# A transformer-style block in fp32: the second normalisation as a factor per token on the turned first one

## The chip, the cores and the metric

The kernel runs on one core of one Trainium2 chip. The metric is the device time of one execution in microseconds (us), as the median of several runs. A core has five instruction streams that run beside each other and meet only at semaphores: PE (matmuls; PEld is its loading of weights), DVE (vector work), ACT (activations, copies), POOL (a second vector engine, without access to the matmul accumulators in PSUM) and SP, which here issues every transfer (DMA). Each stream runs its instructions strictly in order, so an instruction that waits holds up everything behind it on its engine.

## The reference, cut to what matters

The shapes are 2048 tokens, 512 features, 32 heads of 16, a window of 256 keys and 1792 hidden features.

```python
def _layernorm(x, axis=-1, eps=1e-5):
    m = jnp.mean(x, axis=axis, keepdims=True)
    v = jnp.var(x, axis=axis, keepdims=True)
    return (x - m) / jnp.sqrt(v + eps)

x  = A_x
xn = _layernorm(x)
s  = attention(xn, A_wqkv, window=256) @ A_wo          # causal, softmax over 256 keys
y  = _layernorm(xn)                                    # a second normalisation, of xn
h  = gelu(y @ B_w1 + B_b1)                             # 512 -> 1792
g  = silu(h @ B_w2 + B_b2)                             # 1792 -> 512
out = x + s * g
```

Since xn has mean 0 and variance v/(v+eps) for each token, y is xn times one number per token, 1/sqrt(v/(v+eps)+eps).

## The kernel before, in words

Matmuls run in fp32 split into a high and a low part: a product is three matmuls (high·high, high·low, low·high), and so every operand exists twice, as `hi` and `lo`. The normalised input is kept turned (features on partitions, tokens along the row) in one big tile, `big[:, part, kt, token]`, named xnT in the profile: part 0 is high, part 1 low, kt is the group of 128 features.

**Attention (up to about 426 us).** The heads go in 8 groups of 4 (n = 0 to 7), the keys of a group in 16 blocks. One pass of the loop over `t` (here called slot t) handles key block t: two score matmuls into the one buffer `stb` (named so in the profile, one for p = 1, one for p = 0), an exp of each on ACT into `pt`, two masks of each on POOL (AFFINE_SELECT), the row maximum for a block 12 slots later (`xy` on PE, then COPY_PREDICATED and TENSOR_REDUCE on DVE), and the product with the values (`zo<-pt,vt`) of the block before. From slot 116 on there are no maxima left, and the scores of p = 1 go to the buffer `xy`. The pairs of `stb` matmuls can be counted from the first at 62.20 us, two a slot, which gives the time at which each slot starts.

Other matmuls are hung into the slots by a table of numbers: `tandem(t0, t1, one, two)` lays two products of 512 columns, each cut into 64-row halves, over the slots t0 to t1, and they end in the two banks `fb`. These are the projections of the later head groups (`pair_qk`, shown as fb<-xnT,wqb), the values of the second half (`pair_v`), and ten of the fourteen hidden blocks of the first 512 tokens (`pair_h`, f = 6 to 13, 2 and 3). `at(t, ...)` puts an instruction into slot t, and `behind(t, ...)` at its end. Each engine's order is the order in which the code issues.

**The second normalisation.** The tokens go through the second half of the block in four chunks of 512. For chunk 0, `open_y` fetches xn back from DRAM (written there as `xn_d` at the start), `y_steps` take statistics and scale in slots 77 to 89, and `y_turn` turns the four tiles on PE in slots 91 and 92 (16 transposes) and splits them. For chunk 1, xn comes back from `xn_d`; for chunks 2 and 3 the input x is loaded again and normalised twice. These three are turned by DVE in 32x32 blocks (STREAM_TRANSPOSE), written to `z_d` and fetched back in pieces of 128 bytes.

**The MLP (426.6 us on).** Chunk c multiplies hidden blocks f with `w2` into four accumulators `acc`. For each f in `activate`, ACT takes the gelu, ACT casts it to its high part `gh` and DVE subtracts to get the low part `gl`; there are two buffers of each, so the cast for f waits for the end of PE's product of f-2. In chunk 1 PE alternates product i-1 with hidden block i+3 in step i, 5.44 us a step, until the hidden blocks run out after step 10; then products 10, 11, 12 and 13 follow each other in 2.72 us each. In steps 10 to 13 DVE and ACT also build the inputs for chunks 2 and 3 (`second_y`: seven sums and differences of the two chunks, which are then multiplied by seven combinations of `w1`: a Strassen-like scheme). From 568 us the two last chunks run.

Of the kernel before, what the change touches and what calls it, by code (L numbers as in the profile page):

```python
# [9 lines left out]
F32 = mybir.dt.float32  # L10
# [40 lines left out]
def mixer_kernel(ctx, tc, x, wqk, wv, wo, w1, b1, w2, b2, out):  # L51
# [7 lines left out]
    small = ctx.enter_context(tc.tile_pool(name="small", bufs=3))  # L59
    dram = ctx.enter_context(tc.tile_pool(name="dram", bufs=1, space=bass.MemoryType.DRAM))  # L60
    attn = ExitStack()
    psum = attn.enter_context(tc.tile_pool(name="psum", bufs=1, space=PSUM))
# [19 lines left out]
    def layernorm(ts, name, on_act, eager=False, n_act=4, by_sums=(), end_act=False, apart=()):  # L82

        n = len(ts)
        nm = small.tile([P, n], F32, tag="nm", name=f"nm{name}") if by_sums else None
        sums = small.tile([P, n, 2], F32, tag="sums", name=f"sums{name}") if by_sums else None

        def total(i):

            nc.scalar.activation(x23[:, 8], ts[i], AF.Identity, accum_out=sums[:, i, 0:1])
            nc.gpsimd.tensor_scalar(nm[:, i: i + 1], sums[:, i, 0:1], -1.0 / D, None, op0=ALU.mult)

        def squares(i):

            nc.scalar.activation(x23[:, 8], ts[i], AF.Square, bias=nm[:, i: i + 1], accum_out=sums[:, i, 1:2])
            ve = small.tile([P, 1], F32, tag="ve1", name=f"ve{name}_{i}")
            nc.gpsimd.tensor_scalar(ve, sums[:, i, 1:2], 1.0 / D, EPS, op0=ALU.mult, op1=ALU.add)  # L100
            nc.gpsimd.tensor_tensor(rs[:, i: i + 1], ve, mhalf[:, :1], op=ALU.pow)
# [7 lines left out]
        mv = small.tile([P, n, 2], F32, tag="mv", name=f"mv{name}")  # L109
        rs = small.tile([P, n], F32, tag="rs", name=f"rs{name}")  # L110
        sh = small.tile([P, n], F32, tag="shift", name=f"shift{name}")

        def each(i):

            stats(i)
            ve = small.tile([P, 1], F32, tag="ve1", name=f"ve{name}_{i}")
# [8 lines left out]
        def shift(i):  # L125
            nc.vector.scalar_tensor_tensor(sh[:, i: i + 1], mv[:, i, 0:1], -1.0, rs[:, i: i + 1],
                                           op0=ALU.mult, op1=ALU.mult)

        def stats(i):
            st = small.tile([P, 6], F32, tag="bn", name=f"bn{name}_{i}")  # L130
            nc.vector.bn_stats(st, ts[i])
            nc.vector.bn_aggr(mv[:, i], st)

        def invert():
            ve = small.tile([P, n], F32, tag="ve", name=f"ve{name}")
            nc.vector.tensor_scalar(ve, mv[:, :, 1], EPS, None, op0=ALU.add)
            nc.gpsimd.tensor_tensor(rs, ve, mhalf[:, :n], op=ALU.pow)

        def shift_all():
            if on_act:  # L140
                nc.vector.scalar_tensor_tensor(sh, mv[:, :, 0], -1.0, rs, op0=ALU.mult, op1=ALU.mult)

        def apply(i, on_act=on_act):
            if on_act:
                nc.scalar.activation(ts[i], ts[i], AF.Identity, bias=sh[:, i: i + 1], scale=rs[:, i: i + 1])
            else:
                nc.vector.tensor_scalar(ts[i], ts[i], mv[:, i, 0:1], rs[:, i: i + 1],
                                        op0=ALU.subtract, op1=ALU.mult)

        def end(i):  # L150

            if i < n_act:
                shift(i)
            apply(i, i < n_act)
        if eager:
            return [(lambda i=i: total(i), lambda i=i: squares(i), lambda i=i: end_sums(i)) if i in by_sums else
                    (lambda i=i: each(i), lambda i=i: end(i)) for i in range(n)]
        return [lambda i=i: stats(i) for i in range(n)] + [invert, shift_all] + [lambda i=i: apply(i) for i in range(n)]
# [23 lines left out]
    xn_d = dram.tile([8, P, D], F32, name="xn_d")  # L182
# [6 lines left out]
    z_d = dram.tile([NCH - 1, 4, P, 512], F32, name="z_d")  # L189
# [48 lines left out]
    b1s = const.tile([P, NF], F32, name="b1s")  # L238

# [123 lines left out]
    def pair_qk(n, c):  # L363
# [11 lines left out]
        def finish(ps, t, copy):  # L375
# [18 lines left out]
            free = t if (n, c) == (1, 2) else max(t + 1 + 2 * (c % 2), 16 * n - 28 + 4 * c)  # L394
            free += 2 * (t == 90)
# [29 lines left out]
    def pair_h(f):  # L425
# [98 lines left out]
    def max_rows(n, c, t):  # L524

        mt = mts.pop((n, c))
        mh = small.tile([P, 2, 2, 2, 4], F32R, tag="mh", name=f"mh_{n}_{c}")
# [4 lines left out]
        mT = small.tile([P, 32], F32, tag="mT", name=f"mT_{n}_{c}")  # L532
# [71 lines left out]
    def open_y():  # L604

        t = bigp.tile([P, 4, 512], F32, tag="wa", name="y0")
        mlp["y"] = [t[:, i] for i in range(4)]
        for i in range(4):
            nc.sync.dma_start(mlp["y"][i], xn_d[i])
        mlp["ln"] = layernorm(mlp["y"], "C0", False)  # L610
# [5 lines left out]
    W1_AREA = {6: 6, 7: 8, 8: 10, 9: 12, 10: 14, 11: 1, 12: 3, 13: 5, 2: 7, 3: 9, 0: 11, 1: 13, 4: 15}  # L616

    def open_yy():
        yh = bigp.tile([P, 2, 512], F32R, tag="wb0", name="yh")
        mlp["yy"] = ([yh[:, 0], yh[:, 1], area(4)[:, 0:512], area(4)[:, 512:1024]],  # L620
                     [area(j)[:, 512 * k: 512 * (k + 1)] for j in (0, 2) for k in range(2)])

    def open_w1():
        mlp["w1"] = bigp.tile([P, 2 * 512], F32R, tag="wb1", name="w1_5")

    def w1_part(a, f):
        at = area(W1_AREA[f]) if f in W1_AREA else mlp["w1"]
# [35 lines left out]
    def y_steps(a, b):  # L663
        run(mlp["ln"][a:b])

# [4 lines left out]

    def y_turn(kt):

        for i in range(4):
            nc.tensor.transpose(fb[kt % 2][:, P * i: P * (i + 1)], mlp["y"][i][:, P * kt: P * (kt + 1)], ident)
        split(mlp["yy"][0][kt], mlp["yy"][1][kt], fb[kt % 2])
# [31 lines left out]
    ln = layernorm(xs[0], "A0", True, True, 3)  # L707
# [8 lines left out]
    ln1 = layernorm(xs[1], "A1", True, True, 2, by_sums=(0, 1), end_act=True, apart=(3,))  # L716
    ln2 = layernorm(xs[2], "A2", True, True, by_sums=(0,))
    ln3 = layernorm(xs[3], "A3", True, True, by_sums=range(4))
# [14 lines left out]
    for i in range(8):  # L733
        behind(-14 + i // 4, nc.sync.dma_start, xn_d[i], xs[i // 4][i % 4])
# [20 lines left out]
    for n, spans in enumerate((((9, 14), (15, 19)), ((20, 24), (25, 30)), ((31, 35), (36, 41)), ((42, 47), (48, 53, 51)),  # L755
                               ((75, 79), (80, 84)), ((85, 90), (93, 98))), 2):
# [4 lines left out]
    for f, *span in ((6, 99, 104, 102), (8, 105, 110), (10, 111, 115), (12, 116, 121, 118, 119), (2, 122, 127, 124, 125)):  # L761
# [13 lines left out]
    at(88, open_yy)  # L775
    for kt in range(KT):
        fills.setdefault((91 + kt // 2, kt % 2), []).append((y_turn, (kt,)))
# [4 lines left out]
    at(99, open_w1)  # L782
    for f, t in ((6, 91), (7, 91), (8, 92), (9, 94), (10, 94), (11, 99), (12, 99), (13, 101), (2, 101), (3, 103), (0, 103),
                 (1, 105), (4, 105), (5, 107)):
        at(t, fetch, "w1", f)
    for f, t, lo_at, lo_by in ((6, 94, 95, nc.vector), (7, 95, 97, on_pool), (8, 96, 98, on_pool), (9, 97, 99, nc.vector),
                               (10, 100, 102, nc.vector), (11, 102, 103, nc.vector), (12, 103, 105, on_pool),
                               (13, 105, 106, on_pool), (2, 106, 108, nc.vector), (3, 107, 109, on_pool),
                               (0, 108, 110, on_pool), (1, 109, 112, nc.vector), (4, 111, 113, on_pool),
# [18 lines left out]
    def first_h(f):  # L808
# [4 lines left out]
        (nc.scalar.copy if f else nc.vector.tensor_copy)(ready[f], fb[f])  # L813
# [93 lines left out]

    def load_y(c):
        return load_x(c, ((mlp["yp"], "y"),), "y")

    def turn_y(c, tiles):

        for i in tiles:
            y = mlp["y"][i]
            nc.vector.transpose(y, y)
            nc.sync.dma_start(z_d[c - 1, i], y)

    def fetch_y(c, kt, dst):

        for k in range(4):  # L920
            at = z_d[c - 1, 0, 0, 128 * kt + 32 * k: 128 * kt + 32 * k + 32]
            nc.sync.dma_start(dst[32 * k: 32 * k + 32].rearrange("p (t j) -> p t j", j=32),
                              bass.AP(tensor=at.tensor, offset=at.offset, ap=[[512, 32], [32 * 512, 16], [1, 32]]))
# [38 lines left out]
    def end_chunk(c, accs, os_, between):  # L962
# [10 lines left out]
        for i in range(4):  # L973
# [16 lines left out]
            else:  # L990
                for q in range(2):
# [9 lines left out]
    halves_of = {("11", 0): 11, ("11", 1): 13, ("21", 0): 7, ("21", 1): 9, ("22", 0): 15, ("t1", 0): 6, ("t3", 0): 8,  # L1001
                 ("t2", 0): 10, ("t4", 0): 12, ("22", 1): 14, ("t1", 1): 1, ("t3", 1): 3, ("t2", 1): 5, ("t4", 1): 4}
# [349 lines left out]
```

## Time and profile before

| what | value |
|---|---|
| median of 3 runs | 738.41 us (738.13 to 738.72) |
| the profiled execution | 738.76 us, span of its core 737.0 us, granted clock 0.999 |
| busy | PE 98%, DVE 69%, ACT 60%, POOL 40% of the span |
| attention up to | 426.57 us (first `acc` matmul) |
| chunk 0 | 426.57 to 480.97 us |
| chunk 1 | 480.97 to 568.01 us |
| chunks 2 and 3 | 568.01 us to the end |

The span is the time from the core's first instruction to its last; 1.8 us lie around it. In the rows below a time is in us from the span's start. In a row of the timeline the first number is the start, the second the length, `x4` says that four like instructions are merged, and the bracket gives the idle time of that engine before it and what ended it. Line numbers are all L43, since one helper issues everything; the names of the tiles tell the work apart.

### The profile page before, as it was taken

Reading aid. Unit: us, or ns where it says so; the run is one execution under the profiler, and the core shown is the slowest. Engines: PE = TensorE matmul, PEld = TensorE weight load, DVE = VectorE, ACT = ScalarE, POOL = GpSimd, SP = SyncE. Lnnn points to the kernel's source line nnn. Section 1 sums busy time; section 2 is a strip of 40 time slices with the busy share of each in tenths; the row PEclk is TensorE's granted clock in tenths of the full one; section 3 lists DMA queues with packets and bytes.
Section 4 is the critical chain, followed back from the end, with each engine's and each line's share of the span. In section 5 each row is a group of like instructions: output and inputs, shape, how many; then the busy total and the mean of one; then the engine's idle time right before and its main releaser. Section 6 shows DMA issues by size and latency. Waiting matters only on the chain.

```text
span 737.0 us, 18757 instructions
## 1 busy us (share of the span) xinstructions
PE 724.7 (98%) x7360; PEld 585.3 (79%) x7360; DVE 511.2 (69%) x790; ACT 444.1 (60%) x744; POOL 298.4 (40%) x644
## 2 busy tenths in 40 slices
PE   8999999999999999999999999999999999999997
PEld 7886777777878887777776688888888888888886
DVE  7886777877776778887772677656667855667823
ACT  7757777878777676788877756443643734541001
POOL 7413757867666565767877600120002000001102
PEclk9999999999999999999999999999999999999999
DMA  8633356766565525747724397747452322253701
GB/s 292 194 65 78 83 145 168 191 169 184 148 151 144 159 72 150 177 124 190 206 82 144 115 324 187 186 125 209 107 107 104 114 68 86 64 180 120 248 19 57
DMA packets 84697, 105.71 MB, mean 143 GB/s; under 512 B 37312, under 2 KB 37568, under 8 KB 84608
## 3 DMA queue, kind: packets, MB, share of 16 engines
q1 hardware_dynamic: 84608, 104.51, 50.5%
q8 instruction: 58, 0.95, 0.5%
q14 instruction: 31, 0.25, 0.1%
HBM read 54.53 MB, written 32.77 MB: 118 GB/s over the span
## 4 chain that ended last, share of the span: by engine, by line
PE 92%; ACT 3%; DVE 2%; DMA 1%; POOL 1%; issue 0%; SPq 0%; DVEq 0%; ACTq 0%
PE acc L43 21%; PE fb L43 19%; PE zo L43 13%; PE p L43 9%; PE stb L43 9%; PE s L43 6%; PE h L43 6%; PE xy L43 5%; PE pv L43 3%; ACT pt L43 3%; POOL pt L43 1%; DMA wvr<-in_wv_dram 1%; DVE xy L43 1%; DVE mt L43 1%; SPq L43 0%
## 5 line engine op out<-in xcount | busy, mean ns | idle before, releaser
L43 POOL TENSOR_SCALAR_AFFINE_SELECT pt<-pt 128x256 f32<-128x256 f32 x480 | 193.6, 428 | 126.0 <-ACT pt L43 123.5
L43 ACT ACTIVATE pt<-stb 128x768 f32<-128x768 f32 (+1 forms) x244 | 188.7, 773 | 42.7 <-PE stb L43 35.9
L43 DVE TENSOR_REDUCE mt<-xy 128x4 f32<-128x1024 f32 (+1 forms) x128 | 152.6, 1192 | 4.4
L43 DVE COPY_PREDICATED xy<-upper,zo 128x512 f32<-128x512 int32 x112 | 77.8, 695 | 69.0 <-PE xy L43 61.5
L43 POOL TENSOR_TENSOR xo<-xo,gated 128x512 f32<-128x512 f32 x15 | 19.9, 1330 | 234.9 <-DVE gated L43 195.8
L43 PE MATMUL fb<-xnT,wqb 64*128 64x512 f32 (+1 forms) x684 | 106.6, 397 | 0.0
L43 PE MATMUL zo<-pt,vt 128*17 128x128 f32 x2880 | 103.7, 275 | 0.3 <-POOL pt L43 0.3
L43 PE MATMUL stb<-qk 64*128 64x384 f32 (+1 forms) x488 | 95.3, 385 | 4.4 <-ACT pt L43 2.9
L43 PE MATMUL acc<-w,gh 128*128 128x512 f32 x320 | 98.5, 389 | 0.0
L43 PEld LDWEIGHTS stb<-qk 64*128 64x128 f32 x488 | 45.7, 183 | 48.8 <-ACT pt L43 39.4
L43 PEld LDWEIGHTS zo<-pt,vt 128*17 128x17 f32 x2880 | 67.5, 97 | 15.6 <-issue 5.0
L43 PEld LDWEIGHTS fb<-xnT,wqb 64*128 64x128 f32 (+1 forms) x684 | 64.4, 185 | 8.4 <-issue 0.6
L43 PEld LDWEIGHTS acc<-w,gh 128*128 128x128 f32 x320 | 60.1, 188 | 12.5
L43 PE MATMUL acc<-w,gl 128*128 128x512 f32 x160 | 62.3, 389 | 0.0
L43 PE MATMUL xy<-qk 64*128 64x256 f32 (+2 forms) x536 | 58.5, 291 | 0.2 <-DVE mt L43 0.2
L43 ACT COPY oraw<-zo 128x128 f32<-128x128 f32 x108 | 28.7, 266 | 39.1 <-PE zo L43 26.6
L43 PEld LDWEIGHTS xy<-qk 64*128 64x128 f32 x536 | 46.7, 185 | 7.0 <-issue 3.1
L43 ACT ACTIVATE gated<-acc 128x512 f32<-128x512 f32 x16 | 8.7, 596 | 59.3 <-DVE acc L43 59.3
L43 PE MATMUL s<-wos,ohl 128*128 128x512 f32 (+1 forms) x204 | 44.3, 377 | 0.0
L43 PEld LDWEIGHTS s<-wos,ohl 128*128 128x128 f32 x204 | 36.8, 188 | 7.1
L43 PEld LDWEIGHTS zo<-qk 64*128 64x128 f32 x448 | 37.5, 185 | 5.3 <-DVE xy L43 2.0
L43 ACT COPY p<-p 128x512 f32<-128x512 f32 x21 | 12.3, 585 | 48.6 <-PE p L43 41.2
(190 smaller groups left out, 1242.5 us busy)
## 6 DMA issues: line engine op xcount, KB each, us to landing
qk<-sh SPq DMA_DIRECT2D x128, 128.0 KB
qk<-pjr SPq DMA_DIRECT2D x64, 128.0 KB
oT_d<-oraw SPq DMA_DIRECT2D x32, 256.0 KB
w_d<-in_w_dram SPq DMA_DIRECT2D x14, 512.0 KB
x<-in_x_dram SPq DMA_DIRECT2D x16, 256.0 KB
or<-oT_d SPq DMA_DIRECT2D x16, 256.0 KB
w<-rden_d SPq DMA_DIRECT2D x16, 256.0 KB
xo<-in_x_dram SPq DMA_DIRECT2D x16, 256.0 KB
```

The source lines that it names most:

```text
L43: r = issue(*args, **kwargs)
```

## The change

The second normalisation is no longer computed from data. `mvs`, `sums` and `rss` keep the statistics of the first one for all 16 tiles of 128 tokens. `scale_parts` makes of them one factor per token with small POOL instructions in slots 54 to 70, DVE turns the 128x32 table in slot 72, it goes to DRAM as `s_d` and comes back spread over all partitions as `scales` (512 tokens along the row). The turned first normalisation in `big` is used as the input of `w1` directly:

- chunk 0 stays where it is in `big`; `w1`'s products are multiplied by `scales` when they leave PSUM. In the attention stage that takes the place of a copy for f = 12, 13, 2, 3, 0 and 1 (on DVE); f = 6 to 11 are copied as before and multiplied on POOL after the attention stage; f = 4 and 5 get a DVE multiplication.
- chunk 1: both parts of `big` are written to DRAM by 12 transfers of 512 KB for chunks 1 to 3 (`keep_xt`, slots 25 to 69), and fetched back; each of the 14 hidden blocks gets a DVE multiplication before its gelu.
- chunks 2 and 3: high and low part are fetched, added on POOL (`join`) and multiplied on DVE (`scale`).

All statistics, scalings and turnings of the second normalisation, the transfers of `xn_d` and `z_d`, and the reloading of x for chunks 2 and 3 are gone. The two slots of the transposes fall out, and the table is written anew: the products of head groups 6 and 7 and the first hidden blocks move by up to one slot, and each pair of them from slot 80 to 115 now takes six slots. `w1`'s parts lie at other places of `big`.

On PE, slot 91, row by row. `qk` are the head group's rows, `ident` the identity that turns, `pt` and `vt` probabilities and values. Before:

```order
L43 MATMUL stb<-qk_695 128x384 x2
L43 MATMUL xy<-qk_91 128x256 x4
L43 MATMUL fb_108<-ident,y_4661 128x128 x4
L43 MATMUL stb<-qk_695 128x384 x2
L43 MATMUL fb_109<-ident,y_4661 128x128 x4
L43 MATMUL zo<-qk_91 128x128 x4
```

and now:

```order
L43 MATMUL stb<-qk_682 128x384 x2
L43 MATMUL xy<-qk_94 128x256 x4
L43 MATMUL fb_111<-xnT,wqb_4973 128x512
L43 MATMUL fb_112<-xnT,wqb_4973 128x512
L43 MATMUL fb_111<-xnT,wqb_4973 128x512
L43 MATMUL fb_112<-xnT,wqb_4973 128x512
L43 MATMUL fb_111<-xnT,wqb_4973 128x512
L43 MATMUL fb_112<-xnT,wqb_4973 128x512
L43 MATMUL stb<-qk_682 128x384 x2
L43 MATMUL zo<-qk_94 128x128 x4
```

The eight transposes of the slot have gone, and the last six half products of a projection pair stand there.

On DVE, steps 12 and 13 of chunk 1 (`gl` is the low part of a gelu, `yt` and `y_21` are the sums and differences for the last chunks, xnT the places they are split to). Before:

```order
L43 TENSOR_TENSOR yt_1_8300<-xnT,gated 128x512
L43 TENSOR_TENSOR gl_12_8317<-g_12_8314,gh_12_8316 128x512
L43 TENSOR_TENSOR xnT<-xnT 128x512
L43 TENSOR_TENSOR xnT<-yt_0_8298,xnT 128x512
L43 TENSOR_TENSOR xnT<-xnT 128x512
L43 TENSOR_TENSOR xnT<-yt_1_8300,xnT 128x512
L43 TENSOR_TENSOR y_21_7959<-y_21_7959,yt_0_8298 128x512
L43 TENSOR_TENSOR y_21_7959<-y_21_7959,yt_1_8300 128x512
L43 TENSOR_TENSOR gl_13_8349<-g_13_8346,gh_13_8348 128x512
```

and now:

```order
L43 TENSOR_TENSOR yt_1_8121<-yh_3_8020,gated 128x512
L43 TENSOR_TENSOR g_12_8135<-h_12_8041,scales 128x512
L43 TENSOR_TENSOR gl_12_8139<-g_12_8135,gh_12_8138 128x512
L43 TENSOR_TENSOR xnT<-yh_2_8017,xnT 128x512
L43 TENSOR_TENSOR xnT<-yt_0_8119,xnT 128x512
L43 TENSOR_TENSOR xnT<-yh_3_8020,xnT 128x512
L43 TENSOR_TENSOR xnT<-yt_1_8121,xnT 128x512
L43 TENSOR_TENSOR y_21_7816<-y_21_7816,yt_0_8119 128x512
L43 TENSOR_TENSOR y_21_7816<-y_21_7816,yt_1_8121 128x512
L43 TENSOR_TENSOR g_13_8168<-h_13_8091,scales 128x512
L43 TENSOR_TENSOR gl_13_8172<-g_13_8168,gh_13_8171 128x512
```

Ahead of each `gl` now stands the multiplication by `scales`, whose result ACT's gelu of the same f reads.

On POOL, slot 54 (`pt_6_1` and `pt_6_0` are the masks of that slot). Now:

```order
L43 AFFINE_SELECT pt_6_1_3489<-pt_6_1_3489 128x2x128 x2
L43 MEMSET sv 128x32
L43 TENSOR_SCALAR sv<-sums 128x1 x7
L43 COPY sv<-mvs 128x4
L43 COPY sv<-mvs 128x2
L43 COPY sv<-mvs 128x3
L43 AFFINE_SELECT pt_6_0_3528<-pt_6_0_3528 128x2x128 x2
```

Before, the two masks stood next to each other; eleven small instructions have come between them.

The core of the diff:

```diff
@@ finish of pair_h
-            copy(raw, ps)
+            if 5 < f < 12:
+                copy(raw, ps)
+            else:
+                nc.vector.tensor_mul(raw, ps, scales)
@@ instead of open_y
+    def scale_parts():
+        def variance():
+            nc.gpsimd.memset(sv, 0.0)
+            for i in range(4 * NCH):
+                if i in squared:
+                    nc.gpsimd.tensor_scalar(sv[:, i: i + 1], sums[:, i, 1:2], 1.0 / D, None, op0=ALU.mult)
...
+        def ratio():
+            for _ in range(2):
+                nc.gpsimd.tensor_tensor(sv[:, 0: 4 * NCH], sv[:, 0: 4 * NCH], rss, op=ALU.mult)
+            nc.gpsimd.tensor_scalar(sv[:, 0: 4 * NCH], sv[:, 0: 4 * NCH], EPS, None, op0=ALU.add)
+        def power(c):
+            at = sv[:, 4 * c: 4 * c + 4]
+            nc.gpsimd.tensor_tensor(at, at, mhalf, op=ALU.pow)
+    def keep_xt(c, kt):
+        nc.sync.dma_start(xt_d[c - 1, kt], big[:, :, kt, 512 * c: 512 * (c + 1)].bitcast(F32))
-    def y_turn(kt):
-        for i in range(4):
-            nc.tensor.transpose(fb[kt % 2][:, P * i: P * (i + 1)], mlp["y"][i][:, P * kt: P * (kt + 1)], ident)
-        split(mlp["yy"][0][kt], mlp["yy"][1][kt], fb[kt % 2])
@@ the table
-                               ((75, 79), (80, 84)), ((85, 90), (93, 98))), 2):
+                               ((75, 79), (80, 85)), ((86, 91), (92, 97))), 2):
...
-    at(74, open_y)
-    for i, t in enumerate((77, 78, 81, 82, 83, 83, 85, 86, 87, 89)):
-        at(t, y_steps, i, i + 1)
...
+    at(54, variance)
+    at(56, ratio)
+    for c in range(NCH):
+        at(58 + 4 * c, power, c)
+    at(72, nc.vector.transpose, svT, sv)
...
+    for k in range(KT * (NCH - 1)):
+        behind(25 + 4 * k, keep_xt, 1 + k // KT, k % KT)
@@ after the attention stage
-    mlp["y"] = [load(mlp["yp"], "y", xn_d[4 + i], f"y_1_{i}") for i in range(4)]
+        for k in range(2 if f < 12 else 0):
+            nc.gpsimd.tensor_tensor(t[:, k], t[:, k], scales, op=ALU.mult)
@@ chunk 1 onwards
+    def fetch_xt(c, kt, dst):
+        nc.sync.dma_start(dst, xt_d[c - 1, kt, :, 1])
+        kept["high", c, kt] = load(mlp["yp"], "y", xt_d[c - 1, kt, :, 0], f"yh_{c}_{kt}")
+    def join(c, kt, dst):
+        to = kept.pop(("high", c, kt))
+        nc.gpsimd.tensor_tensor(to if c > 2 else dst, dst, to, op=ALU.add)
...
+    def scale(c, dst):
+        nc.vector.tensor_mul(dst, dst, gated[:, c - 2])
@@ activate
+            if f not in made:
+                nc.vector.tensor_mul(g, src, scales)
+                src = g
             nc.scalar.activation(g, src, AF.Gelu_apprx_tanh, bias=b1s[:, f: f + 1])
@@ steps of chunk 1
+                if i == 9:
+                    for kt in range(KT):
+                        join(3, kt, kept["y3", kt])
+                        scale(3, kept["y3", kt])
```

More of the change, by code (lines that the diff above doesn't have):

```diff
@@ L123, in power, with apply @@
             nc.gpsimd.tensor_tensor(rs[:, i: i + 1], ve, mhalf[:, :1], op=ALU.pow)
[L125 to L143, printed above, removed]
+        def apply(i, on_act):
             if on_act:
@@ L152, in end @@
             if i < n_act:
-                shift(i)
+                nc.vector.scalar_tensor_tensor(sh[:, i: i + 1], mv[:, i, 0:1], -1.0, rs[:, i: i + 1],
+                                               op0=ALU.mult, op1=ALU.mult)
             apply(i, i < n_act)
[L155 to L158, printed above, removed]
+        return [(lambda i=i: total(i), lambda i=i: squares(i), lambda i=i: end_sums(i)) if i in by_sums else
+                (lambda i=i: each(i), lambda i=i: end(i)) for i in range(n)]
     def run(steps):
@@ L812, in first_h @@
         ready[f] = t2.tile([P, 512], F32, tag="t2", name=f"hf_{f}")
-        (nc.scalar.copy if f else nc.vector.tensor_copy)(ready[f], fb[f])
+        nc.vector.tensor_mul(ready[f], fb[f], scales)
     ready = {}
@@ L1182, in mixer_kernel @@
                     for kt in range(KT):
[L1183 removed]
+                        fetch_xt(2, kt, kept[kt // 2][:, kt % 2])
+                    for k in range(2):
+                        fetch_scales(2 + k, gated[:, k])
+                if i in (5, 6):
+                    for kt in (2 * i - 10, 2 * i - 9):
+                        join(2, kt, kept[kt // 2][:, kt % 2])
+                if i in (7, 8):
+                    for kt in (2 * i - 14, 2 * i - 13):
+                        scale(2, kept[kt // 2][:, kt % 2])
                 if i in (8, 9):
```

176 lines of the change are left out of this document (75 added, 101 removed).

## The prediction

> **What bounds the kernel now.** I read the page's busy shares and its chain of waits first, then the busy time by stretches, then the chain in order of time, and at last the timelines of the places that the change touches.
>
> ```profile
> span 737.0 us, 18757 instructions
> PE 724.7 (98%) x7360; PEld 585.3 (79%) x7360; DVE 511.2 (69%) x790; ACT 444.1 (60%) x744; POOL 298.4 (40%) x644
> PE 92%; ACT 3%; DVE 2%; DMA 1%; POOL 1%; issue 0%; SPq 0%; DVEq 0%; ACTq 0%
> ```
>
> PE carries the chain, so the stages have to be looked at one by one. The chain from the MLP on:
>
> ```profile
> 527.21 2.72 PE h L43 x12
> ...
> 546.25 10.88 PE acc L43 x48
> ```
>
> and the busy time by stretches (columns: PE, PEld, DVE, ACT, POOL, granted clock, DMA share, GB/s):
>
> ```profile
> 62.00:275.73 213.73, 210.80 (x3352) 166.92 (x3350) 153.68 (x191) 159.05 (x267) 142.05 (x338) 1.00 0.55 143
> 426.57:480.97 54.40, 54.40 (x241) 45.06 (x241) 37.78 (x64) 29.97 (x49) 4.89 (x4) 1.00 0.76 222
> 480.97:568.01 87.04, 87.04 (x385) 72.10 (x385) 58.44 (x112) 42.88 (x68) 9.87 (x8) 1.00 0.51 134
> ```
>
> PE has not one gap in chunk 0 (54.40 us) and chunk 1 (87.04 us). There is nothing to win there by taking work from DVE, ACT or the transfers; such work can only be put in PE's way. Everything to be won lies in the attention stage. The slots there start with the first of two `stb` rows. The six starts below are those of slots 36, 54, 80, 98, 110 and 115; the other two rows are the transposes of slot 91.
>
> ```profile
> 165.93 0.44 PE L43 MATMUL stb<-qk 64*128 64x384 f32 x2 [0.20 <-ACT pt L43]
> 215.32 0.44 PE L43 MATMUL stb<-qk 64*128 64x384 f32 x2
> 290.23 0.44 PE L43 MATMUL stb<-qk 64*128 64x384 f32 x2
> 322.04 0.66 PE L43 MATMUL fb<-ident,y 128*128 128x128 f32 x4
> 323.16 0.66 PE L43 MATMUL fb<-ident,y 128*128 128x128 f32 x4
> 341.85 0.45 PE L43 MATMUL stb<-qk 64*128 64x384 f32 x2 [0.16 <-ACT pt L43]
> 375.19 0.38 PE L43 MATMUL stb<-qk 64*128 64x256 f32 x2
> 389.43 0.46 PE L43 MATMUL stb<-qk 64*128 64x384 f32 x2
> ```
>
> **The attention stage: the table.** Slots 80 to 114 (35 slots) take 389.43 - 290.23 = 99.20 us, 2.83 us each: the five or six slots of a pair are unevenly loaded, two of them hold transposes, and DVE and POOL do the second statistics. Afterwards each pair there takes six slots, which hold 8, 8, 8, 8, 10 and 6 half products. Before, slots 36 to 53 have that load three times over with nothing else in them: (215.32 - 165.93) / 18 = 2.744 us each. Slots 98 to 109 have it but for one slot's shift, with the preparation of `w1` beside it: (375.19 - 341.85) / 12 = 2.778 us. If all 35 slots go at 2.744, they take 96.04 us and 3.2 us are won. If slots 92 to 114, where `w1` is prepared, go at 2.778, it is 12 x 2.744 + 23 x 2.778 = 96.82, and 2.4 us are won. I take the middle, **-2.8 us**. The 16 transposes are part of this and not added to it.
>
> **The end of the attention stage.** At slot 121 ACT copies h of f = 12; now DVE multiplies it. The chain there:
>
> ```profile
> 405.35 0.47 ACT hr L43
> 405.83 0.73 ACT pt L43
> 406.61 0.86 POOL pt L43
> 412.98 0.41 PE zo L43 x8
> ```
>
> ACT's copy lies on the chain with 0.47 us, ahead of an exp and of a run of masks which ends at 412.98. It moves to DVE, where a multiplication out of PSUM follows another; the new wait would be PE's for the second bank, whose first use is in slot 122. I take **-0.4 us**, between 0 (the masks end as late) and -0.5. At slot 127 DVE was idle, and a second multiplication of some 0.7 us there, and those of f = 0 and 1, cost nothing as long as PE's twelve matmuls between them cover them.
>
> **POOL in slots 54 to 70.** The factors cost eleven small instructions in slot 54, three in 56, and four powers of 128x4.
>
> ```profile
> L43 POOL TENSOR_TENSOR rsC<-veC,mhalf 128x4 f32<-128x4 f32 x5 | 5.5, 1102 | 46.1 <-DVE veC L43 46.1
> L43 POOL TENSOR_SCALAR nmA<-sumsA 128x1 f32<-128x1 f32 x7 | 1.5, 223 | 7.1 <-ACT x L43 7.1
> 218.11 0.77 POOL L43 TENSOR_SCALAR_AFFINE_SELECT pt<-pt 128x256 f32<-128x256 f32 x2 [0.66 <-ACT pt L43]
> 220.85 0.95 PE zo L43 x28
> ```
>
> Eleven times 0.22 us is 2.45 us. POOL was idle 0.66 us before the masks at 218.11, so they slip by 1.8 us, from an end at 218.88 to 220.7. The first to wait for them is PE's `zo` at 220.85, whose last third alone reads them: **0 us**, and at most 0.5 if the small ones follow each other at 0.28. A power of 1.1 us exceeds such a pause by 0.5 us in a slot with as much slack again.
>
> **Transfers.** 12 x 512 KB leave in slots 25 to 69 (121 us at 2.74 a slot), 52 GB/s on top of the 143 at a share of 0.55. The head groups' rows that share SP's queue and the lanes are sent ten slots or more ahead of their use from group 3 on, and SP waits for nothing new there, so **0 us**; if one landing came late, its lateness would be the price, at most 2 us by the length of a transfer of this size. Gone are the eight writes of xn at the start; no chain ran through them, 0 us. In chunk 0, four loads of 512 KB replace sixteen of 128-byte pieces, and DVE and ACT lose their splits: nothing, since PE had no gap.
>
> ```profile
> 443.95 0.72 ACT L43 ACTIVATE g<-hr,b1s 128x512 f32<-128x512 f32 x1
> L43 POOL TENSOR_TENSOR xo<-xo,gated 128x512 f32<-128x512 f32 x15 | 19.9, 1330 | 234.9 <-DVE gated L43 195.8 <-DMA xo<-in_x_dram 37.2 <-issue 1.9
> ```
>
> The six POOL multiplications of f = 6 to 11 (1.33 us each by the row `xo`, 8 us from about 431 us on) end before the first gelu that needs them, at 443.95 us, unless the tiles land 4 us late.
>
> **Chunk 1, the tail.** Here the change adds 14 multiplications to DVE's queue, each ahead of the gelu of the same f, and eight multiplications for the last chunks. Steps with hidden blocks have 5.44 us of PE work; there they hide under PE. In steps 11 to 13 PE has only 2.72 us a step. DVE, ACT and PE there before:
>
> ```profile
> 533.16 0.69 DVE L43 TENSOR_TENSOR gl<-g,gh 128x512 fp32r<-128x512 f32 x1 [2.35 <-ACT gh L43]
> 533.76 1.29 DVE L43 TENSOR_TENSOR xnT<-y,xnT 128x512 fp32r<-128x512 f32 x2
> 538.60 0.69 DVE L43 TENSOR_TENSOR gl<-g,gh 128x512 fp32r<-128x512 f32 x1 [3.54 <-ACT gh L43]
> 549.49 0.69 DVE L43 TENSOR_TENSOR gl<-g,gh 128x512 fp32r<-128x512 f32 x1 [1.15 <-ACT gh L43]
> 552.51 1.29 DVE L43 TENSOR_TENSOR y<-y,yt 128x512 f32<-128x512 f32 x2
> 553.71 0.69 DVE L43 TENSOR_TENSOR gl<-g,gh 128x512 fp32r<-128x512 f32 x1
> 548.83 0.62 ACT L43 CAST gh<-g 128x512 fp32r<-128x512 f32 x1 [2.16 <-PE acc L43]
> 551.44 0.68 ACT L43 ACTIVATE g<-h,b1s 128x512 f32<-128x512 f32 x1
> 554.25 0.62 PE L43 MATMUL acc<-w,gh 128*128 128x512 f32 x2
> 554.70 0.39 PE L43 MATMUL acc<-w,gl 128*128 128x512 f32 x1
> ```
>
> The `gl` of f = 13 was ready at 553.71 + 0.69 = 554.40, 0.3 us before PE's first use of it at 554.70. So PE had almost no cover left. Gelu and cast of f = 13 were done on ACT while DVE was still busy with the sums. Now gelu 13 waits for a multiplication that stands behind those sums on DVE. Two like DVE instructions take 1.29 us, so one follows another in 0.605 us. A multiplication that is followed by gelu, cast and `gl` takes 0.69 + 0.68 + 0.62 + three handovers of 0.04 (549.45 to 549.49 is one), 2.11 us from its start to that of `gl`. DVE now, from the `gl` of f = 9 at 533.16, which PE still sets:
> - `gl` 9, two splits, four multiplications of chunk 3: 7 x 0.605, so multiplication 10 starts at 537.40 and `gl` 10 at 539.51 (before 538.60);
> - five on, multiplication 11 at 542.53 and `gl` 11 at 544.64;
> - seven on, multiplication 12 at 548.88 and `gl` 12 at 550.99, before PE needs it;
> - seven on, multiplication 13 at 555.22, cast 13 done at 557.29, `gl` 13 at 557.33, done at 558.02.
>
> PE's last product can start at 557.3, not 554.25, and 0.45 us later it waits 0.27 us more for `gl`: **+3.3 us**. Nothing behind it gives this back, since PE goes on without a gap and all its suppliers slip by as much. If DVE kept its old times up to `gl` 11 it would be 2.7.
>
> Queued on DVE behind the multiplications of chunk 3 is all of this, and they wait for POOL's additions of the parts (`join`). The last of them needs a transfer into the place of `w1`'s block 10, free at the end of PE's hidden block 10 at 527.21 + 2.72 = 529.93. With 3.5 us for two transfers and an addition it is done at about 534.8; DVE asks for it at 536.8.
>
> ```profile
> 399.31 3.06 POOL L43 TENSOR_SCALAR_AFFINE_SELECT pt<-pt 128x256 f32<-128x256 f32 x8 [1.08 <-ACT pt L43]
> 406.61 10.54 POOL L43 TENSOR_SCALAR_AFFINE_SELECT pt<-pt 128x256 f32<-128x256 f32 x19 [0.37 <-ACT pt L43]
> 409.19 0.77 DVE L43 TENSOR_TENSOR w<-w 128x512 fp32r<-128x512 f32 x1
> ```
>
> A mask took 3.06 / 8 = 0.38 us alone and 10.54 / 19 = 0.55 us while DVE split `w2`; DVE's subtraction took 0.77 for 0.69. So POOL and DVE hold each other up, POOL the more. I take the additions as free. The Trainium skill, page "SBUF — State Buffer", section "SBUF: two separate sides", speaks against that: a DVE instruction with two SBUF inputs and a POOL instruction that reads SBUF need the same port pair, and the one that comes second is blocked for the whole of the other. By that rule an addition that starts under DVE's run could hold it by 1.33 us and the sum would come out at 739.8 us; the rows above agree in kind, not in size.
>
> **The sum.** -2.8 - 0.4 + 0 + 0 + 3.3 = +0.1 us on the profiled execution's 738.76, so 738.86. That execution is 0.35 us above the median of 738.41, so the median should come to **738.5 us**. A change of 0.2%, 1.48 us, is about what measurements of this kernel can tell from none.
>
> **The rivals.**
> - *The tail hides the multiplications* (faster). The stall falls away if DVE reaches multiplication 13 by 554.25 - 2.07 = 552.2, 3.0 us earlier than by my list. For it speaks DVE's busy share of 67% in chunk 1 (58.44 of 87.04) and the pause of 3.54 us at 538.60; against it, that the list already uses up that pause. Then 738.5 - 3.3 = 735.2 us.
> - *The parts of chunk 3 come late* (slower). One mechanism: DVE waits at the multiplications of chunk 3 for POOL's additions and these for the transfers into `w1`'s place. From 536.8 on each us of lateness moves `gl` 13 by as much; it decides at 1.4 us of lateness. For it speaks that eight transfers of 256 KB share the stretch with the rest at a share of 0.51; against it, 2 us of slack. With the last landing 4 us late the stall grows by 2 to 2.5 us, 740.8 us.
> - *The even table gives little* (slower too, at the edge). If slots under 12 half products are held by the pair of `stb` matmuls and exps in turn, not by PE's load, only the transposes count, two slots shorter by some 0.7 us. Then -1.4 in place of -2.8 and 739.9 us; slots 98 to 109 at 2.778, hardly above 2.744, speak against more than half of that.
>
> **How the numbers follow.** My sum holds with 0.53, the hidden tail with 0.25, the late parts with 0.14 and the weak table with 0.08. The bounds of the sum's terms (2.4 to 3.2, 0 to 0.5, 0 to 0.5, 2.7 to 3.3) give 737.4 to 739.4 for the likeliest case alone. The range has to reach the hidden tail with the first two terms at their best (735.2 - 0.5 = 734.7) and the late parts with the second term at its worst (740.8 + 0.4 = 741.2, the copy not off the chain): 734.7 to 741.2. Faster by over 0.2% is the hidden tail, 0.25; slower the late parts and most of the weak table, 0.2; the rest, 0.55, lies within.
>
> **What would show it.** Slots 80 to 114 at about 96.4 us in all; no PE wait at `zo` in slots 54 and 55; `gl` 13 starting about 3 us later against PE's end of product 12, PE idle there for some 3 us with ACT's `gh` named, and chunk 1 at 90 us in place of 87.04. I am wrong if chunk 1 is still 87.0 us, if DVE waits for POOL in front of chunk 3's multiplications, or if chunk 0, which I cost at nothing, is longer than 54.4 us.

## The result

The changed kernel takes **747.39 us** (median of 4 runs, 747.30 to 747.54) beside 738.57 us (738.13 to 739.66) for the kernel before on the same chip: a ratio of 1.0117 (95% interval 1.010 to 1.0135), 8.8 us slower. I forecast 738.5 us and a range up to 741.2. The profiled execution took 747.43 us with a span of 745.7 us.

The page of the changed kernel, busy shares and chain by engine:

```profile
span 745.7 us, 18574 instructions
PE 728.3 (98%) x7344; PEld 583.7 (78%) x7344; DVE 498.2 (67%) x736; ACT 425.2 (57%) x713; POOL 316.7 (42%) x669
PE 89%; DVE 4%; ACT 4%; issue 1%; DMA 1%; SPq 0%; POOL 0%; DVEq 0%; ACTq 0%
```

PE has 16 matmuls less (the transposes), and yet is busy 3.6 us longer; and DVE and ACT now own 8% of the chain. The stages of the changed kernel, by stretches with the columns of the prediction: chunk 0, chunk 1, the last chunks, and the end of chunk 1 by itself.

```profile
424.73:480.15 55.42, 55.42 (x241) 45.09 (x241) 31.96 (x49) 21.96 (x36) 11.46 (x9) 1.00 0.59 183
480.15:575.07 94.92, 91.10 (x386) 72.98 (x385) 57.09 (x86) 32.71 (x52) 17.43 (x12) 0.98 0.38 117
575.07:745.70 170.63, 166.06 (x738) 136.72 (x737) 103.49 (x183) 53.13 (x90) 10.60 (x8) 1.00 0.34 105
552.00:564.00 12.00, 8.18 (x26) 5.56 (x26) 9.54 (x17) 6.61 (x12) 0.00 (x0) 0.86 0.23 67
```

The last chunks of the kernel before, which the prediction did not need:

```profile
568.01:737.00 168.99, 164.71 (x738) 136.71 (x737) 103.62 (x183) 53.12 (x90) 10.69 (x9) 1.00 0.34 106
```

So the attention stage ends 1.84 us earlier (424.73 against 426.57), chunk 0 takes 1.02 us more, chunk 1 7.88 us more, and the last chunks, in which the change touches nothing, 1.64 us more. These add up to the 8.7 us of the two spans. Chunk 0 and the last chunks have as many matmuls as before. PE has no gap in chunk 0, and in the last chunks it is busy 1.35 us longer (166.06 against 164.71): the matmuls themselves are slower. The chain in order of time shows which:

```profile
424.73 5.44 PE acc L43 x24
438.43 30.80 PE acc L43 x132
480.15 10.89 PE h L43 x48
...
559.25 4.88 PE acc L43 x12
...
575.07 19.05 PE p L43 x84
594.12 5.60 PE acc L43 x24
691.97 38.09 PE acc L43 x168
```

The 132 `acc` matmuls of chunk 0 took 29.92 us and now take 30.80: three of them 0.70 us in place of 0.68. The hidden blocks (10.89 for 48, before 10.88) and the `p` of the last chunks (19.05, before 19.04 for 84) keep their pace, and so do the `acc` matmuls that read no `gh` and `gl`: the last 168 (38.09, before 38.08), whose inputs are split into `big`, and the first 24 of chunk 0 (5.44 as before), which load their weights from the tile `g_first`.

In chunk 1 there is a second loss. PE, from the timeline:

```profile
552.91 0.73 PE L43 MATMUL acc<-w,gh 128*128 128x512 f32 x2 [0.80 <-ACT gh L43]
555.84 0.40 PE L43 MATMUL acc<-w,gl 128*128 128x512 f32 x1
559.25 0.74 PE L43 MATMUL acc<-w,gh 128*128 128x512 f32 x2 [3.01 <-ACT gh L43]
561.38 1.05 PE L43 MATMUL acc<-w,gh 128*128 128x512 f32 x2
562.23 0.63 PE L43 MATMUL acc<-w,gl 128*128 128x512 f32 x1
562.66 1.05 PE L43 MATMUL acc<-w,gh 128*128 128x512 f32 x2
...
563.94 2.28 PE L43 MATMUL s<-wos,ohl 128*128 128x512 f32 x9
```

PE waits 0.80 us for f = 12 and 3.01 us for f = 13. After the second wait three `acc` matmuls take 562.66 - 561.38 = 1.28 us instead of 0.70, and the granted clock of these 12 us is 0.86. The whole group of twelve takes 4.88 us where 2.80 would be its pace (the row of 559.25 in the chain). Some eight of the twelve go at half pace, 0.43 us from one to the next. DVE and POOL ahead of it:

```profile
527.64 0.69 DVE L43 TENSOR_TENSOR gl<-g,gh 128x512 fp32r<-128x512 f32 x1 [3.05 <-ACT gh L43]
528.25 2.38 DVE L43 TENSOR_TENSOR y<-y,gated 128x512 f32<-128x512 f32 x2
530.55 2.38 DVE L43 TENSOR_TENSOR xnT<-gated,xnT 128x512 fp32r<-128x512 f32 x2
532.86 0.68 DVE L43 TENSOR_TENSOR g<-h,scales 128x512 f32<-128x512 f32 x1
534.98 0.69 DVE L43 TENSOR_TENSOR gl<-g,gh 128x512 fp32r<-128x512 f32 x1 [1.45 <-ACT gh L43]
557.11 0.68 DVE L43 TENSOR_TENSOR g<-h,scales 128x512 f32<-128x512 f32 x1
559.23 0.69 DVE L43 TENSOR_TENSOR gl<-g,gh 128x512 fp32r<-128x512 f32 x1 [1.44 <-ACT gh L43]
```

```profile
527.97 1.51 POOL L43 TENSOR_TENSOR yh<-xnT,yh 128x512 f32<-128x512 f32 x1 [9.59 <-DMA yh<-xt_d]
530.19 1.59 POOL L43 TENSOR_TENSOR yh<-xnT,yh 128x512 f32<-128x512 f32 x1 [0.71 <-DMA yh<-xt_d]
```

Two pairs of DVE instructions that should take 1.29 us took 2.38 each, and under each pair lies one of POOL's additions of chunk 3's parts.

### The profile page after: what moved, and what is told of

Same layout as the page of the kernel before. It is cut to its first block, busy times and chain, and to the rows that moved or that the text cites. A ratio compares the mean times of both kernels' runs of the same rounds, so it can differ in the third digit from the quotient of the medians.

```text
span 745.7 us, 18574 instructions
## 1 busy us (share of the span) xinstructions
PE 728.3 (98%) x7344; PEld 583.7 (78%) x7344; DVE 498.2 (67%) x736; ACT 425.2 (57%) x713; POOL 316.7 (42%) x669
## 4 chain that ended last, share of the span: by engine, by line
PE 89%; DVE 4%; ACT 4%; issue 1%; DMA 1%; SPq 0%; POOL 0%; DVEq 0%; ACTq 0%
PE fb L43 19%; PE acc L43 19%; PE zo L43 13%; PE p L43 9%; PE stb L43 9%; PE s L43 6%; PE xy L43 6%; PE h L43 4%; PE pv L43 3%; ACT pt L43 2%; DVE xnT L43 1%; DVE xy L43 1%; DMA x<-in_x_dram 1%; ACT gh L43 1%; ACT g L43 0%
## 5 line engine op out<-in xcount | busy, mean ns | idle before, releaser
L43 PE MATMUL acc<-w,gh 128*128 128x512 f32 x320 | 101.9, 400 | 3.8 <-ACT gh L43 3.8
L43 PE MATMUL acc<-w,gl 128*128 128x512 f32 x160 | 64.2, 401 | 0.0
L43 PE MATMUL p<-xnT 128*128 128x512 f32 x189 | 51.9, 390 | 0.0
L43 DVE TENSOR_TENSOR gl<-g,gh 128x512 fp32r<-128x512 f32 x24 | 17.3, 723 | 42.7 <-ACT gh L43 42.7
```

Source lines behind the costliest of these rows:

```text
L43: r = issue(*args, **kwargs)
```

## The experiments

Three suspects: where `gh` and `gl` lie (for the slower `acc`), DVE's order with POOL's additions (for the waits), and the pause itself (for the half pace). The kernels below are compared with the kernel before on the same chip (738.5 to 738.8 us).

**Without the filler tile.** Before the change the program puts `big` at byte 17664 of a partition, the halves of `w2` at 83200 and 115968, `gh` at 193792: all 256 past a multiple of 512. (These are the addresses of the built program.) A filler tile of 320 bytes ahead of `gh`, `gl`, `ohl` and `wos` brings that about. The change adds the 2048 bytes of `scales` ahead of `big` and takes the pool of small tiles away from behind `t2`; `big`, `w2` and `g_first` stay at 256 past, but `gh` comes to 194112, 64 past. The edit:

```diff
-    ctx.enter_context(tc.tile_pool(name="pad", bufs=1)).tile([P, 80], F32, name="pad")
```

> The changed kernel without its 320-byte filler tile, so that gh, gl, ohl and wos lie again at 256 bytes past a multiple of 512 in a partition, as big and w2 do (with the filler they lie at 64 past). Theory (the place sets the pace): three matmuls of an acc product take 0.68 us again instead of 0.70, so 42 groups of twelve get 0.08 us each back, 3.4 us, and the s groups some 0.2; of the 1.1 us of that in chunk 1 nothing is won, since PE only waits longer for gl of f = 13 there. About 745.0 us, chunk 0 at 54.4 us. Rival (DVE, POOL or transfers that run beside PE slow its matmuls): no difference, 747.4 us, chunk 0 at 55.4 us.

Measured: 744.58 us (ratio to before 1.0072, 1.0057 to 1.0087), chunk 0 back at 54.40 us, the 132 matmuls at 29.92 us, as the theory has it. PE's waits in chunk 1 are now 1.32 and 3.03 us:

```profile
438.63 29.92 PE acc L43 x132
557.82 0.73 PE L43 MATMUL acc<-w,gh 128*128 128x512 f32 x2 [3.03 <-ACT gh L43]
```

One of its four executions took 742.64 us at a granted clock of 1.0, the other three 744.6 at 0.998. The difference of 2 us is what the half pace costs, so that execution probably went without it; it has no trace.

**The kernel before, with only the place changed.**

```diff
-    ctx.enter_context(tc.tile_pool(name="pad", bufs=1)).tile([P, 80], F32, name="pad")
+    ctx.enter_context(tc.tile_pool(name="pad", bufs=1)).tile([P, 32], F32, name="pad")
```

> The kernel before with the filler tile cut from 320 to 128 bytes, so that gh, gl, ohl and wos lie at 64 bytes past a multiple of 512, and big and w2 stay at 256. No instruction differs. Theory (the place sets the pace): acc groups of twelve at 2.80 us instead of 2.72 in chunks 0 to 2, 42 x 0.08 = 3.4 us and 0.2 for s: 742.0 us. Rival (the instructions beside PE slow it): 738.5 us.

Measured: 742.54 us, 3.76 us more than the kernel before beside it (ratio 1.005, 1.0035 to 1.0065). No instruction differs; the place alone does it.

**The kernel before, with everything shifted together.**

```diff
+    ctx.enter_context(tc.tile_pool(name="pad0", bufs=1)).tile([P, 80], F32, name="pad0")
     bigp = ctx.enter_context(tc.tile_pool(name="bigp", bufs=1))
```

> The kernel before with a filler of 320 bytes ahead of everything big, so that big, w2 and the t2 tiles move to 64 bytes past a multiple of 512 together with gh, gl, ohl and wos. No instruction differs. If what slows a product is that its two operands lie differently to 512 bytes: 738.8 us, three acc matmuls 0.68 us. If it is that an operand lies off 256 at all: 742.5 us or more, three acc matmuls 0.70 us.

Measured: 738.49 us (ratio 0.9999, 0.999 to 1.0008). `gh` lies at 194112 here too, its place in the changed kernel, and nothing is lost. The chain of this kernel, and then of the one with only `gh` shifted:

```profile
440.05 29.92 PE acc L43 x132
```

```profile
439.92 30.80 PE acc L43 x132
```

So it is not the own place of `gh` that counts but how it lies to the tiles that were shifted with it. In all these kernels the matmuls whose two operands lie on the same side of the filler keep their pace: the hidden blocks, the `acc` matmuls from `g_first`, and `s` with `wos` and `ohl` (48 in 10.92 us against 10.88). The reading that fits them all is the distance between the two operands of a matmul: the columns of `gh` or `gl` that are loaded as weights and the rows of `w2` that stream past. A distance that is a multiple of 512 bytes costs nothing; one that is 320 past such a multiple costs 0.02 us in three matmuls. Other distances were not tried, and why the distance matters stays open.

**The multiplications earlier.** In chunk 1 the multiplication of f + 1 is issued ahead of the gelu of f, and so ahead of `second_y`'s sums:

```diff
         for i in range(NF + 1):
+            for f in ([0, 1] if i == 0 else [i + 1]) if c else ():
+                if f < NF:
+                    multiply(f, hs.pop(f))
             if i < NF:
                 activate(order[i])
             if c and i >= 10 and i < 14:
                 second_y(i - 10)
```

> The changed kernel with one thing moved: in chunk 1 the multiplication by scales of f + 1 stands on DVE ahead of the gelu of f, and so ahead of second_y's sums, not behind them. Theory (DVE's order makes the tail's stall, and the stall the slow matmuls after it): gl of f = 13 is ready at about 554.0 + 0.7 us, PE has no wait in chunk 1 and no matmuls at half pace after it; 0.8 + 3.0 us of waits and some 2.3 us of slow matmuls go, 741.2 us. Rival (DVE has too much work in these steps in any order): the stall shrinks by no more than a multiplication or two, 745.5 to 747 us.

Measured: 741.26 us (ratio 1.0034, 1.0021 to 1.0047), and PE has no gap in chunk 1:

```profile
480.65:569.13 88.48, 88.48 (x385) 72.13 (x385) 59.81 (x86) 32.08 (x52) 16.37 (x12) 1.00 0.39 125
```

DVE is busier than in the changed kernel (59.81 against 57.09 us, with the same 86 instructions), so it was its order, not its load, that held PE up. The waits and the half pace go together.

**Without POOL's additions for chunk 3** (the low part of that chunk's input is left out):

```diff
     def join(c, kt, dst):
         to = kept.pop(("high", c, kt))
-        nc.gpsimd.tensor_tensor(to if c > 2 else dst, dst, to, op=ALU.add)
+        if c < 3:
+            nc.gpsimd.tensor_tensor(dst, dst, to, op=ALU.add)
```

> The changed kernel without POOL's four additions of chunk 3's parts (the low part of that chunk's input is left out). Theory (a POOL addition that overlaps a DVE instruction on SBUF holds DVE up): the multiplications of chunk 2's second half take 1.29 us for two instead of 2.38, and the two subtractions behind them 1.29 instead of 2.38, so all of DVE's queue from gl of f = 9 on is 2.2 us earlier, and PE's waits for f = 12 and 13 fall from 3.8 to about 2.3 us: 745.0 to 745.9 us. Rival (something else, a transfer or ACT's copies, stretches these four): 2.38 us each pair as before and 747.4 us.

Measured: 744.39 us (ratio 1.0083, 1.0066 to 1.010), a little less than expected. DVE in this kernel:

```profile
528.26 1.29 DVE L43 TENSOR_TENSOR y<-y,gated 128x512 f32<-128x512 f32 x2
529.47 1.29 DVE L43 TENSOR_TENSOR xnT<-gated,xnT 128x512 fp32r<-128x512 f32 x2
533.20 0.69 DVE L43 TENSOR_TENSOR gl<-g,gh 128x512 fp32r<-128x512 f32 x1 [1.84 <-ACT gh L43]
```

and PE at its one wait:

```profile
557.49 0.73 PE L43 MATMUL acc<-w,gh 128*128 128x512 f32 x2 [2.56 <-ACT gh L43]
558.55 0.63 PE L43 MATMUL acc<-w,gh 128*128 128x512 f32 x2
```

Each pair takes 1.29 us when no addition runs under it: an addition cost DVE 1.09 us, twice. (Without the filler tile two additions lie under one pair, which takes 3.48 us: 1.1 for each again.) The `gl` of f = 9 starts at 533.20, 1.78 us earlier, and PE's waits shrink from 3.81 to 2.56 us. After 2.56 us the matmuls keep their pace (0.63 for two); in one of the four executions, at 746.0 us and a granted clock of 0.997 against 0.999 in the others, they seem not to have. That the pace was kept is probably why the time lies under the expectation, which had counted the half pace in.

**A pause in the kernel before.** Six more subtractions on DVE ahead of `gl` 13:

```diff
                 put("t2", k, kept["t2", k])
+                for _ in range(3):
+                    low("t2", k, kept["t2", k])
```

> The kernel before with six subtractions of 128x512 more on DVE (the low parts of t2 made four times over) ahead of the gl of f = 13 in chunk 1, 6 x 0.605 = 3.6 us. PE then stops for some 3.2 us in its last product of chunk 1. If the matmuls at half pace in the changed kernel follow from the pause as such, they stand here too, some ten of them at 0.43 us instead of 0.23, and the time is 738.8 + 3.2 + 2.0 = 744.0 us. If they are something of the changed kernel: 742.0 us.

Measured: 744.35 us, 5.9 us more. PE:

```profile
558.87 0.63 PE L43 MATMUL acc<-w,gl 128*128 128x512 f32 x1 [3.94 <-DVE gl L43]
559.29 1.06 PE L43 MATMUL acc<-w,gh 128*128 128x512 f32 x2
```

The half pace follows from the pause and has nothing to do with the change: 3.9 us of waiting cost 2.0 us more afterwards. The Trainium skill, page "TensorE: Matmul & The Clock Gate", section "Part 1: The HAM clock gate", says that the array falls to half rate after an idle window of some 3.4 us, and that the window runs freely, so that the same pause may or may not fill one. The runs agree in kind. Only one execution of each kernel has a trace; the others are judged by their time and granted clock. By these, every execution of the changed kernel, with its pause of 3.01 us, lost the clock, three of four of the kernel without the filler tile (3.03 us), and one of four of the kernel without the additions (2.56 us). As the trace counts idle time, all three pauses are shorter than the window that the Trainium skill gives. Counted from the start of the last matmul before it (555.84) to the next (559.25), the pause of 3.01 us is 3.41 us; the runs do not show which count decides.

**Both repairs**: no filler tile and the early multiplications.

> The changed kernel without its filler tile and with the early multiplications. If the place of the tiles and the order on DVE are the two causes and independent of each other, it takes 741.3 - 3.6 = 737.7 us, 0.15% under the kernel before; PE without a gap from 425 us on, chunk 0 at 54.4, chunk 1 at 87.0, the rest at 169.0 us. Rival: PE, 1.1 us faster in chunk 1, catches up with gl of f = 12 or 13 again: 738.5 to 740 us.

Measured: 737.39 us (ratio 0.9986, 0.9977 to 0.9994). PE runs chunk 1 without a gap again, and at the old pace:

```profile
424.72:479.12 54.40, 54.40 (x242) 45.06 (x241) 32.95 (x49) 22.02 (x36) 12.05 (x9) 1.00 0.59 186
479.12:566.16 87.04, 87.04 (x386) 72.10 (x385) 59.72 (x86) 32.00 (x52) 17.09 (x12) 1.00 0.41 127
```

Against the kernel before on the same chips the changed kernel stands at +8.8 us, with early multiplications at +2.5, with both repairs at -1.1. The order on DVE thus cost 6.3 us, the place 3.6, and what is left of the change wins 1.1. Repaired in the other order (the place first, +5.8) the place cost 3.0 and the order 6.9: while PE waits for DVE in chunk 1, a faster PE there only waits longer.

**The table.** How much of that is the even table? First only its spans as before, in the kernel with early multiplications:

```diff
-  ((75, 79), (80, 85)), ((86, 91), (92, 97))), 2):
+  ((75, 79), (80, 84)), ((85, 90), (93, 98))), 2):
...
-  (6, 98, 103), (8, 104, 109), (10, 110, 115),
+  (6, 99, 104, 102), (8, 105, 110), (10, 111, 115),
```

> The kernel with early multiplications, and in it the table as before for slots 80 to 115 (pairs of five and six slots, a gap where the transposes stood, the fetches of w1 from f = 11 on one slot later). By the prediction's first term the even pairs are worth 1.4 us of the 2.8, so 742.7 us. By what slots 80 to 114 took (97.53 us, against 99.20 less 1.4 for the transposes) the table itself is worth 0.3 us: 741.6 us.

Measured: 744.10 us, +5.6 against the kernel before where the even table stands at +2.5, and outside both expectations. PE waited 4.6 us for ACT's exps in slots 80 and on, against 1.9 us, probably because the copies on ACT were still timed for the new spans. So this run tells nothing on the spans. Then with all numbers as before, those of the fetches, splits and copies too:

> The kernel with early multiplications, and in it all numbers of the table for slots 80 to 115 as before: the spans, the times of w1's fetches, of its splits, and of the copies of head group 7. The old spans alone came to 744.1 us, with PE waiting 4.6 us for ACT's exps instead of 1.9. If these waits came from ACT copies that fell together because their times belonged to the new spans, they go, and what is left is the worth of the even pairs: 742.7 us by the prediction's 1.4 us, 741.6 us if nearly nothing.

Measured: 740.98 us (ratio 1.0035, 1.0022 to 1.0048), +2.5 against the kernel before, as with the even table. Slots 80 to 115 in it, from the first row's start to the second's:

```profile
290.30 0.44 PE L43 MATMUL stb<-qk 64*128 64x384 f32 x2
387.68 0.44 PE L43 MATMUL stb<-qk 64*128 64x384 f32 x2
```

97.38 us, against 99.20 before the change. Slots 91 and 92, which held the transposes, from the first row of 91 to that of 93, before the change:

```profile
321.43 0.44 PE L43 MATMUL stb<-qk 64*128 64x384 f32 x2
328.35 0.44 PE L43 MATMUL stb<-qk 64*128 64x384 f32 x2
```

and in this run:

```profile
321.35 0.44 PE L43 MATMUL stb<-qk 64*128 64x384 f32 x2
326.77 0.44 PE L43 MATMUL stb<-qk 64*128 64x384 f32 x2
```

6.92 us against 5.42: 1.5 of the 1.8 us. The even pairs are worth nothing; the two slots without transposes are nearly the whole gain.

**The small terms.** The kept transfers issued twice, in the kernel with early multiplications:

```diff
-        nc.sync.dma_start(xt_d[c - 1, kt], big[...])
+        for to in (xt_d, xt2_d):
+            nc.sync.dma_start(to[c - 1, kt], big[...])
```

> The kernel with early multiplications, with each of the 12 transfers of 512 KB that keep the turned normalisation issued twice, to two places. The prediction costed the 12 at nothing; then 12 more cost nothing: 741.3 us. If the 0.28 us by which slot 39 is longer than before (3.03 against 2.75 us) come from SP's queue, which each of them lengthens by 0.56 us, other slots are hit too: 741.6 to 743 us.

Measured: 740.61 us (ratio 1.0031, 1.0019 to 1.0042); slot 39 is 3.04 us as with twelve. Twelve more cost nothing, and SP's queue is not what lengthens slot 39; its 0.28 us, which every kernel with the change has, are not explained.

The copy of f = 12 on ACT as before, multiplied on POOL later, in the kernel with both repairs:

```diff
-            if 5 < f < 12:
+            if 5 < f < 13:
...
-        for k in range(2 if f < 12 else 0):
+        for k in range(2 if f < 12 else 1):
```

> The kernel with both repairs, where ACT copies h of f = 12 in slot 121 as before and POOL multiplies it after the attention stage. By the prediction's term this gives the 0.4 us back that the change won there: 737.8 us. By the traces of before and after, slot 121 gets 0.32 us shorter again and slot 124 0.48 us longer: 737.5 us.

Measured: 737.38 us (ratio 0.9986, 0.9977 to 0.9995), the same. Slots 121 and 124, counted from their `stb` rows, are 2.02 and 2.51 us again, as before the change, instead of 2.34 and 2.05: most of what is won at the one is lost at the other.

At last one number of the table, `(10, 101, 102, ...)` to `(10, 100, 102, ...)`, in the kernel with both repairs:

> The kernel with both repairs, where ACT's copy for the high part of w1's block f = 10 is issued in slot 100, not 101, in which ACT also copies the high part of head group 7's last rows. If two ACT copies between two exps make the 3.08 us of slot 101, it falls to about 2.75: 737.1 us. If it is the fetches, nothing changes: 737.4 us.

Measured: 737.02 us (ratio 0.998, 0.9971 to 0.9989), slot 101 at 2.70 us instead of 3.09. Two ACT copies between two exps had made it long. This is the fastest kernel of the study, faster than both that were compared.

## Why the prediction was wrong

The spans differ by 8.7 us where the sum had 0.1. Of these 8.6 us, 1.4 are missing gains of the attention stage (-1.84 instead of -3.2), 4.6 are chunk 1 (+7.88 instead of +3.3, with 1.1 of it from the place of the tiles), and 1.0 and 1.6 are chunk 0 and the last chunks, both taken at nothing.

- *Attention, the table (-2.8 us).* It gave 1.67, and for another reason than I gave. Slots 80 and 115 of the changed kernel start at

```profile
290.16 0.45 PE L43 MATMUL stb<-qk 64*128 64x384 f32 x2
387.69 0.44 PE L43 MATMUL stb<-qk 64*128 64x384 f32 x2
```

  97.53 us instead of 99.20. I had read the gain from slots 36 to 53 with the same load, 2.744 us each. But slots 80, 82 and 84 were long before and stayed so (3.09, 2.97 and 2.95 us), and slot 101 grew to 3.08 us by the ACT copies that the new table brought together. The run with the whole old table shows that evening out the load per slot wins nothing there. This is the rival that the even table gives little; its 1.4 us for the transposes were close.
- *The end of attention (-0.4).* The copy off ACT gave next to nothing: slots 115 to 126 take 29.33 us, before 29.44. The chain shows the wait that I named and costed at zero:

```profile
404.14 0.69 DVE hr L43
404.84 0.04 issue
404.88 0.96 PE fb L43 x6
```

  PE's next product cannot enter the second bank until DVE's second multiplication has emptied it.
- *POOL's factors (0).* Right: slots 54 and 55 take 3.24 and 3.17 us, before 3.23 and 3.19; no `zo` waits there.
- *Transfers (0).* Right as far as the runs show: doubled, they cost no more. What makes slot 39 longer by 0.28 us is open.
- *Chunk 0 (0).* Wrong: 55.42 us instead of 54.40. The sum had no term for it, nor for the 1.64 us of the last chunks. I argued that without a gap on PE nothing can be lost, and took PE's own pace as fixed. It was not: the change moved tiles, and the distance between operands sets that pace. No row of the profile before showed it; the code did, in a filler tile whose size fits the old layout alone.
- *Chunk 1, the tail (+3.3).* The mechanism was right and the list almost exact from its start on: it had `gl` of f = 9 at 533.16 and of f = 13 at 557.33; they came at 534.98 and 559.23, 1.8 and 1.9 us later. Two steps failed. The first is "the `gl` of f = 9 at 533.16, which PE still sets": DVE set it, since POOL's additions had already held up what stands ahead of its multiplication. I took the additions as free for POOL and so for DVE, although my own rows showed the two holding each other up; here it was DVE that lost, 1.09 us each time. The Trainium skill's rule that I cited, page "SBUF — State Buffer", section "SBUF: two separate sides", was the better guide: the second to come is blocked. I had estimated 1.33 us by it; an addition cost 1.09. The second is "nothing behind it gives this back", which left out that something is added: the pause of 3.0 us is followed by 2.1 us of loss, most of it matmuls at half pace. The waits were 3.81 us in place of 3.3, and 4.35 (1.32 and 3.03) with PE at its old pace; with the half pace and the halts before and after, the runs put the order's price at 6.3 us.
- *The bounds.* Those of the sum's terms add up to 739.8 us at the upper end, not 739.4; the range does not hang on it.
- *The rivals.* "The parts of chunk 3 come late" was near: the parts did hurt DVE, not by coming late but by being added under its work. DVE did not wait for them. "The tail hides the multiplications" is what the early order makes true.

## What to carry to other kernels

Where PE is the bound, its pace is a term of the sum too: when a change adds, removes or moves tiles, compare the distance of the operands that meet in a matmul before and after. A multiplication put ahead of an activation belongs ahead of whatever else its engine does in that step, since everything behind it on three engines waits. And a pause of PE of 3 to 4 us cost about 2 us more than itself here, so of several waits the longest is the one to break up.

## What the runs showed of the hardware

- With `gh` and `gl` at a distance from `w2` that is 320 bytes past a multiple of 512, three `acc` matmuls of 128x512 take 0.70 us instead of 0.68; with both shifted alike they take 0.68. Over this kernel it is 3.8 us.
- Two DVE instructions of 128x512 on SBUF took 2.38 us with one POOL addition of 1.5 us under them, and 1.29 us without.
- After a pause of 3.0 us in an otherwise full stream, some eight matmuls run at 0.43 us instead of 0.23; after one of 2.56 us none in the traced execution.
